# Two mix matmul pairs in place of one behind the operand sums of chunks 4 to 10

## The chip, the cores and the metric

The kernel runs on one core of a Trainium2 chip. Times are device microseconds (us) of one execution. A few executions of each kernel are timed in turn with executions of the kernel before. Kernels with a single timed execution are used for their profiles only. A profile is one further execution, and its times are counted from its first instruction.

Engines are called as the profile calls them: PE (matmuls), PEld (weight loads), DVE (vector engine), ACT (scalar engine), POOL, and SP.

## The reference, cut to what matters

```python
# x: (8, 4224, 192); first a 7-tap causal convolution with softmax weights per head, then:
theta = x @ w_theta
zr, zi = x * np.cos(theta), x * np.sin(theta)
y = einsum('ts,bsd->btd', w_tok_r, zr) + einsum('ts,bsd->btd', w_tok_i, zi)
u = x + y
out = u + np.maximum(u @ w_ch, 0.0)
```

The token mix `einsum('ts,bsd->btd')` is most of the work: 7656 of the 9809 matmuls.

## The kernel before

Tokens are cut into 33 chunks of 128. Each chunk is convolved (PE), copied out of PSUM (ACT), transposed (PE, ACT), multiplied with w_theta (PE), sent through two sine activations (ACT), and made into operands by two products and four sums (DVE). The mix is a stream of pairs of 128x384 matmuls, each pair on one weight tile. The stream consists of steps. A step makes two row blocks of the output from the chunks that are ready (2, 4, 5, 7, 9, then 11), in seven runs that save multiplications in the manner of Strassen and Winograd; the names "11", "S1", "S2", "S4", "S3", "12", "22" are those of the weight tiles.

Chunks 0 to 10 are made at the beginning, in what I call the front. There the stream is not issued in one piece: `between(n)` issues up to n of its pairs between the stages of the chunks.

```python
    for i in range(NW + 2):                 # NW = 11
        ch = chunks.get(i) if i < NW else None
        old = chunks[i - 1] if 0 < i <= NW else None
        ...
        if ch:
            ch.conv(0)
        between(2)
        if old:
            old.theta(0)
        between(1)
        if ch:
            ch.conv(1)
        ...
        ready[0] = i - 2
        between(2)
        if old:
            old.theta(1)
        ...
        between(1)
        if ch:
            ch.transpose()
        if old:
            old.product(Z11)
        between(2)
        ...
        if old:
            old.product(Z21)
        between(1)
        if old:
            old.sums(0)
        between(1)
        if old:
            old.sums(1)
        between(1)
```

The program gives each engine its work in this order of issue. The work that a step of the mix asks of the other engines is issued with its pairs, at positions from 0 to 7 (one per run): weight tiles are turned (L336) and summed (L348) on DVE for the next step, and a finished run is given from PSUM (`y`) to SBUF (`pv`), by a copy on ACT (L406) or an addition on DVE (L408).

```python
    def w_tasks(self):
        ...
            (0.25, lambda: self.turn("11")), (1.2, lambda: self.turn("21")),
            (2.05, lambda: self.wsum("S3")), (2.2, lambda: self.turn("22")),
            (3.05, lambda: self.wsum("S1")), (3.3, lambda: self.wsum("S2")),
            (4.2, lambda: self.turn("12")), (5.1, lambda: self.wsum("S4")),
    ...
    def wtile(self):
        return wpool.tile([P, NW, NQ, Q], F16, name="wt", tag="wt", bufs=9)
    ...
    ypool = ... tc.tile_pool(name="yps", bufs=2, space=bass.MemoryType.PSUM)   # y: 2 tiles of 2 banks
```

Of the kernel before, what the change touches and what calls it, by code (L numbers as in the profile page):

```python
# [16 lines left out]
def kernel(  # L17
# [257 lines left out]
    def load_chunk(k):  # L275
        if k < NK and k not in chunks:
            chunks[k] = Chunk(k, before=chunks[k - 1] if k % NW else None)
# [308 lines left out]
    def idle(n):  # L586
        for _ in range(n):
            pe(nc.tensor.matmul(
                spare[:, 0, 0:BH], lhsT=noise[:, 0:P], rhs=noise, start=True, stop=True
            ))  # L590
# [54 lines left out]
    def more(n):  # L645

        for i in range(n):
            if need[0] is None:
                need[0] = next(flow, NK)
            if need[0] > ready[0]:  # L650
                return n - i
            need[0] = next(flow, NK)
        return 0
# [8 lines left out]
    for i in range(NW + 2):  # L662
        ch = chunks.get(i) if i < NW else None
        old = chunks[i - 1] if 0 < i <= NW else None

        def between(n):
            left = more(n)
            if 0 < i < 3:
                idle(min(left, 2))
# [9 lines that stand above are left out]
        if i == 0:  # L679
            idle(4)  # L680
# [4 lines that stand above are left out]
        if i == 1:  # L685
            for at, f in steps[0].w_tasks():
                if at < 2.2:
                    f()
        if i + 3 < NW:
            load_chunk(i + 3)  # L690
# [6 lines that stand above are left out]
        if i == 1:  # L697
            for at, f in steps[0].w_tasks():
                if at >= 2.2:
                    f()  # L700
        if old:
            old.product(Z21)
        between(1)
        if old:
            old.sums(0)
        between(1)
        if old:
            old.sums(1)
        between(1)
    ready[0] = NK  # L710
    for _ in flow:
        pass
# [31 lines left out]
```

## Time and profile before

| quantity | value | where it is from |
|---|---|---|
| time, median of the first three runs | 1447.86 us (1446.54 to 1449.32) | timed runs |
| span of the profile | 1444.6 us | profile page |
| PE busy | 1414.5 us, 98% | profile page |
| front: from the first theta of chunk 4 to PE's resumption after its last gap | 44.46 to 102.48 us, 58.02 us long | timeline |
| PE busy and DVE busy in that stretch | 51.91 and 51.98 us | table of windows |

The front is the piece that the change touches. It begins with a matmul that stands before the first moved pair, and it ends with a mix matmul that has the same place in PE's order in every kernel (the 774th that is profiled, but for the two kernels that have fewer or more matmuls on purpose).

### The profile page before, as it was taken

The page shows a single profiled execution, that of the slowest core. Times are in us where ns is not written, and L with a number is a line of the kernel's source. Part 1 is how long each engine was busy: PE and PEld are TensorE (multiplying, and loading weights), DVE is VectorE, ACT ScalarE, POOL GpSimd, SP SyncE. Part 2 cuts the span into 40 slices and gives each one's busy share as a digit, 9 for nine tenths or more (in the row PEclk, how much of TensorE's full clock was granted, in tenths as well). Part 3 has the DMA queues.
Part 4 walks back from the last instruction along what each step waited for, and adds up shares of the span by engine and source line. Part 5 has one row for each costly group of instructions (what it writes and reads, how often), then busy time and mean ns, then how long its engine had stood idle before and what let it go on. Part 6 is the DMA issues. An engine that isn't in the chain of part 4 may idle for free.

```text
span 1444.6 us, 23749 instructions
## 1 busy us (share of the span) xinstructions
PE 1414.5 (98%) x9809; PEld 886.3 (61%) x9809; DVE 978.2 (68%) x1050; ACT 316.2 (22%) x379; POOL 434.6 (30%) x655
## 2 busy tenths in 40 slices
PE   7899999999999999999999999999999999999997
PEld 4656666666666666666666666666666666666665
DVE  6893554555448687866666657876877677767686
ACT  6851101111124254000000004435210110010133
POOL 8421211111223232432433343233323123213120
PEclk9999999999999999999999999999999999999999
DMA  9975756564699999897899889989999999898883
GB/s 181 253 148 136 146 119 133 98 152 87 152 229 210 226 244 222 219 265 173 223 245 222 233 155 239 235 181 237 274 220 202 213 204 221 204 200 193 166 232 116
DMA packets 272029, 281.99 MB, mean 195 GB/s; under 512 B 106672, under 2 KB 240176, under 8 KB 271920
## 3 DMA queue, kind: packets, MB, share of 16 engines
q0 software_dynamic: 162464, 92.15, 48.4%
q1 hardware_dynamic: 71824, 178.88, 35.2%
q10 hardware_dynamic: 37632, 9.44, 4.3%
q8 instruction: 77, 1.26, 0.4%
q14 instruction: 32, 0.26, 0.1%
HBM read 245.49 MB, written 108.13 MB: 245 GB/s over the span
## 4 chain that ended last, share of the span: by engine, by line
PE 89%; DVE 3%; DMA 2%; ACT 2%; POOL 1%; issue 1%; SPq 0%; DVEq 0%; ACTq 0%; POOLq 0%
PE y L443 81%; PE v L141 5%; PE pc L210 1%; PE tp L165 1%; ACT z L246 1%; DVE pv L408 1%; DMA xw<-xw 1%; POOL xw L197 1%; DMA xw<-in_x_dram 1%; DVE z L257 1%; POOL st L323 1%; DVE z L251 1%; DMA pv<-part 1%; ACT uT L151 1%; DVE wt L336 0%
## 5 line engine op out<-in xcount | busy, mean ns | idle before, releaser
L443 PE MATMUL y<-z,wt 128*128 128x384 f16 x7656 | 1283.6, 326 | 10.4 <-DVE pv L408 7.3
L443 PEld LDWEIGHTS <-wt 128*128 128x128 f16 x7656 | 740.7, 98 | 488.1 <-issue 10.2
L408 DVE TENSOR_TENSOR pv<-y,pv 128x768 f32<-128x768 f32 x324 | 309.2, 955 | 327.0 <-PE y L443 286.8
L336 DVE STREAM_TRANSPOSE wt<-st 128x1408 f16<-128x1408 f16 (+7 forms) x224 | 327.8, 1465 | 45.8 <-PE y L443 39.1
L323 POOL DMA_DIRECT2D st<-in_moe_w_tok_r_dram x232 | 132.4, 579 | 464.9 <-DVE wt L336 459.4
L323 POOL DMA_DIRECT2D st<-in_moe_w_tok_i_dram x232 | 132.5, 580 | 405.4 <-DVE wt L336 397.5
L348 DVE TENSOR_TENSOR wt<-wt 128x1408 f16<-128x1408 f16 (+7 forms) x216 | 176.1, 815 | 40.5 <-PE y L443 38.0
L151 ACT ACTIVATE z<-pc 128x768 f16<-128x768 f32 x65 | 53.3, 820 | 386.7 <-PE pc L210 386.5
L151 ACT ACTIVATE ub<-pv 128x768 f16<-128x768 f32 x63 | 50.2, 835 | 333.2 <-DVE pv L408 310.7
L406 ACT ACTIVATE pv<-y 128x768 f32<-128x768 f32 x66 | 54.0, 819 | 281.6 <-PE y L443 281.6
L141 PEld LDWEIGHTS <-uT 128*128 128x128 f16 x1056 | 91.1, 98 | 27.4 <-issue 8.5
L386 POOL TENSOR_TENSOR pv<-pv,xr 128x1536 f32<-128x1536 f32 x24 | 74.5, 3105 | 67.1 <-DVE pv L476 21.9
L197 POOL DMA_DIRECT2D xw<-in_x_dram x132 | 76.5, 591 | 30.1 <-DMA xw<-xw 9.7
L476 DVE SCALAR_TENSOR_TENSOR pv<-v,pv 128x768 f32<-128x768 f32 x66 | 62.9, 954 | 27.5 <-PE v L141 27.0
L151 ACT ACTIVATE uT<-tp 128x1536 f16<-128x1536 f16 (+1 forms) x49 | 59.7, 1221 | 74.4 <-PE tp L165 74.4
L257 DVE TENSOR_TENSOR z<-z 128x768 f16<-128x768 f16 x132 | 73.4, 556 | 3.6
L246 ACT ACTIVATE z<-v,half_pi 128x768 f16<-128x768 f32 x66 | 59.9, 907 | 42.1 <-PE v L141 41.7
L251 DVE TENSOR_TENSOR z<-z 128x1536 f16<-128x1536 f16 x66 | 60.1, 948 | 6.6 <-ACT z L246 6.6
L141 PE MATMUL v<-wth,uT 128*128 128x192 f16 x528 | 55.0, 248 | 5.6 <-ACT z L246 3.3
L141 PE MATMUL v<-wch,uT 128*128 128x192 f16 x528 | 54.2, 246 | 2.1 <-DVE pv L476 1.2
L246 ACT ACTIVATE z<-v 128x768 f16<-128x768 f32 x66 | 53.5, 810 | 0.0
L210 PE MATMUL pc<-xw,bands 96*64 96x192 f16 x528 | 35.3, 256 | 1.2 <-DVE bands L628 0.8
(43 smaller groups left out, 138.0 us busy)
## 6 DMA issues: line engine op xcount, KB each, us to landing
part<-pv SPq DMA_DIRECT2D x79, 768.0 KB, 4.6
pv<-part SPq DMA_DIRECT2D x79, 768.0 KB, 6.0
out_dram<-pv SPq DMA_DIRECT2D x66, 384.0 KB, 4.3
st<-in_moe_w_tok_r_dram POOLq DMA_DIRECT2D x136, 176.0 KB, 5.7
st<-in_moe_w_tok_i_dram POOLq DMA_DIRECT2D x136, 176.0 KB, 5.1
xs<-z SPq DMA_DIRECT2D x132, 96.0 KB, 4.1
xw<-in_x_dram POOLq DMA_DIRECT2D x121, 96.0 KB, 5.9
xr<-xs SPq DMA_DIRECT2D x24, 384.0 KB, 4.5
```

The lines of the kernel that those rows point to most:

```text
L141: pe(nc.tensor.matmul(v[:, k, b * D : (b + 1) * D], lhsT=tT[:, 3 * k + b + i, :], rhs=w[:, 2 * b + i, :], start=(i == 0), stop=(i == 1),))
L151: act(nc.scalar.activation(out=out, in_=in_, func=AT.Copy))
L197: nc.gpsimd.dma_start(out=self.xw[lo : lo + n, h, :, :], in_=x[:, t0 : t0 + n, :].rearrange("b s d -> s b d"),)
L246: act(nc.scalar.activation(**args))
L251: dve(nc.vector.tensor_tensor(out=o, in0=xv, in1=o, op=ALU.mult))
L257: dve(nc.vector.tensor_tensor(out=z[:, o, :], in0=z[:, a, :], in1=z[:, b, :], op=ALU.subtract))
L323: pool(nc.gpsimd.dma_start(out=st[a * Q : (a + 1) * Q, 0:nb, :, 0:n] .rearrange("i r bt s -> i (r bt) s"), in_=w[self.tbs[0] * P : (self.t ...
L336: dve(nc.vector.transpose(self.w[name][:, 0 : self.n, :, :], self.st[int(name[1])][:, int(name[0]) - 1, :, 0 : self.n * Q] .rearrange("p b ...
L348: dve(nc.vector.tensor_tensor(out=self.w[name][:, 0 : self.n, :, :], in0=self.w[a][:, 0 : self.n, :, :], in1=self.w[b][:, 0 : self.n, :, : ...
L386: ins = pool(nc.gpsimd.tensor_tensor(out=self.pv[i], in0=self.pv[i], in1=self.xr[i], op=ALU.add))
L408: dve(nc.vector.tensor_tensor(out=o, in0=yv, in1=o, op=ALU.add))
L443: pe(nc.tensor.matmul(y[cn][:, q, 0:BH], lhsT=self.w[wn][:, c, :, :].rearrange("p bt i -> p (bt i)"), rhs=chunks[k].z[:, zn, q * BH : (q + ...
```

## The change

The intent is to fill PE's idle time in the front: while DVE forms the operand sums, PE gets two mix pairs to do in place of one.

```diff
         between(1)
         if old:
             old.sums(0)
-        between(1)
+        between(2 if i > 4 else 1)
         if old:
             old.sums(1)
-        between(1)
+        between(2 if i > 4 else 1)
```

No instruction is added or removed.

## The prediction

> **What bounds the kernel now.** I read the whole-kernel shares first, to see how much there is to win at all.
>
> ```profile
> PE 1414.5 (98%) x9809; PEld 886.3 (61%) x9809; DVE 978.2 (68%) x1050; ACT 316.2 (22%) x379; POOL 434.6 (30%) x655
> PE 89%; DVE 3%; DMA 2%; ACT 2%; POOL 1%; issue 1%; SPq 0%; DVEq 0%; ACTq 0%; POOLq 0%
> ```
>
> PE is busy for 1414.5 of 1444.6 us, so all its idle time is 30.1 us, 2.1% of the span. The change reorders instructions and removes none, so that is the outer ceiling. The second question is how much of it lies where the change acts. That is the front: chunks 0 to 10 are convolved, turned, rotated by theta and multiplied, with mix matmul pairs (two 128x384 matmuls on one weight tile) strewn between. By the timeline, the iteration that makes chunk 5 and finishes chunk 4 has its turn at 47.97 us and the last front theta at 90.58. The table of windows:
>
> ```profile
> 48.00:102.48 54.48, 48.86 (x434) 32.33 (x432) 49.19 (x70) 43.01 (x53) 15.60 (x28) 1.00 0.97 205
> 103.00:1444.60 1341.60, 1328.99 (x9034) 829.64 (x9032) 894.96 (x918) 240.64 (x286) 382.33 (x554) 1.00 0.87 195
> ```
>
> Columns: window, its length, then PE, weight load, DVE, ACT, POOL busy. From 48 to 102.48 us PE is busy 48.86 of 54.48: 5.6 us idle, 0.39% of the run. Everything after 103 us keeps its instructions and order. So only these 5.6 us are in play, and I looked at which waits make them. PE's rows of the timeline (whole ones with a gap over 0.4 us):
>
> ```profile
> 51.92 0.48 PE L443 MATMUL y<-z,wt 128*128 128x384 f16 x2 [0.61 <-ACT pv L406]
> ...
> 61.12 0.48 PE L443 MATMUL y<-z,wt 128*128 128x384 f16 x2 [0.99 <-DVE pv L408]
> ...
> 83.80 0.81 PE L443 MATMUL y<-z,wt 128*128 128x384 f16 x4 [0.48 <-DVE pv L408]
> ...
> 87.32 1.78 PE L443 MATMUL y<-z,wt 128*128 128x384 f16 x10 [0.41 <-DVE pv L408]
> ...
> 102.48 5.70 PE L443 MATMUL y<-z,wt 128*128 128x384 f16 x34 [2.31 <-DVE pv L408]
> ```
>
> Four of the five end with a vector addition that clears a PSUM tile (y), the last and longest one when the front is already over: DVE still works off its backlog and PE waits for it. So near the end of the front the bound is DVE, and I read its rows for idle time:
>
> ```profile
> 57.65 0.84 DVE L336 STREAM_TRANSPOSE wt<-st 128x640 f16<-128x640 f16 x1 [1.42 <-PE y L443]
> ...
> 80.06 1.11 DVE L336 STREAM_TRANSPOSE wt<-st 128x896 f16<-128x896 f16 x1 [1.43 <-PE y L443]
> ...
> 93.72 1.78 DVE L251 TENSOR_TENSOR z<-z 128x1536 f16<-128x1536 f16 x2
> ...
> 101.47 0.95 DVE L408 TENSOR_TENSOR pv<-y,pv 128x768 f32<-128x768 f32 x1
> ```
>
> From 80.06 to 102.34 DVE has no visible gap. Its last gap, 1.43 us, is a wait for the mix itself: the weight turn "12" needs a weight buffer (of nine) that is free only when the mix has ended its S3 run.
>
> [...] DVE and ACT are the front's busy ones (49.2 and 43.0 of 54.5 us, DVE without a gap after 80 us), PE the later bound, and the gaps of 1.42 and 1.43 us are waits for a weight buffer. [...] So a blocked turn "12" holds up all products behind it, as at 80.06, and it is the order that is being changed here. [...]
>
> **The change, part by part.** Added and removed work: none; the listing of both programs has 19620 PE rows each. Moved: one pair later in the stream is issued behind each of two sums, 2 extra pairs for each of chunks 4 to 10. Against the old order, the convolution of chunk 6 comes 2 pairs later, of chunk 7 4, of chunk 10 10, and the last thetas (chunk 10) 12. (The pairs placed after chunk 10's own sums have only mix behind them anyway.) A pair takes 2 x 0.164 us (ten matmuls in the row of 1.79 us less the last one's tail), so 0.33 us, and by the end of the front 12 x 0.33 = 3.9 us of mix has moved ahead of theta. It is not saved; it fills idle PE time or pushes the front later.
>
> (a) What DVE regains. In the new order the turn "12" of the 7-chunk step stands behind the products and two sums of chunk 7, and S3 ends in the chunk 9 iteration right after its first convolution, while in the old order it ended after that iteration's turn of the operand. I estimate S3's end at about 76 us and DVE's arrival at 77.5 (old 78.6, less two sums of 0.56). So the gap of 1.43 us goes, if nothing else delays DVE. The gap of 1.42 us at 57.65 stays: S3 of the step before ends at the same row (850) in both orders.
>
> (b) What DVE loses. Theta comes later, so the sines do, so the products may wait. Chunk 10: the last theta began at 90.58, its last sine ended at 93.6, and DVE took the product at 93.72, so there is hardly any slack. With 3.9 us more mix ahead and about 1.5 of the 3.1 us idle that PE showed in between recovered, theta begins at about 93.0 and the first half's sines are done about 95.2. DVE comes there at 93.72 - 1.43 + 2.05 (a weight sum of 0.75 and a turn of 1.30 now stand ahead of it) = 94.3, and waits about 0.8.
>
> (c) The end of the backlog. After that DVE has two products (1.75), two weight sums (1.54), four sums (2.3) and the addition (0.87), together 6.5 us: 95.2 + 6.5 = 101.7, against 102.34 before. Without the wait of (b) it is 100.9. PE itself arrives earlier (100.17 minus what idle it fills), but it must wait for this addition, because the pair that opens run "12" needs its bank. So PE resumes 0.6 to 1.4 us earlier, and everything behind it shifts by as much. Gain: about 1.0 us, 1447.86 - 1.0 = 1446.8.
>
> **Rivals.**
> 1. PE-bound front: all idle is filled, because the extra pairs stand exactly where PE waits for ACT. For it: 5.6 us idle. Against: 2.3 of these are the DVE backlog, whose work before that addition is the same in both orders, and the waits for y at 61, 83.8 and 87.3 are DVE's too. It would give 1443 to 1444.
> 2. ACT-starved front: the delay of convolution and theta reaches the sines and DVE loses more than (a) gives. For it: ACT already waits for theta (0.6 us at 60.16 and 63.51, 0.85 at 89.80) and DVE's slack at chunk 10 is 0.1 us. Against: the pairs are put at the end of an iteration, where ACT still has sines and a turn of 1.45 us in hand. It would give 1448 to 1450.
> 3. A transfer: one load of x now stands behind a weight load that waits for a turn (issued about 61 in place of 53.6 us, for a convolution after 73). With about 6 us to land and 4.7 for the halo copy it is still in time; no effect.
>
> **Range and chances.** The three runs before spread from 1446.5 to 1449.3, so half of my range is noise. The mechanism allows -4 to +2 us. Range 1443.8 to 1449.6. 2% is 29 us, five times all the idle time in play, so both verdicts beyond it get 1% and "same" gets 98%.
>
> **What would show it.** Right: PE idle from 48 us to the end of the front's backlog is 4 to 5 us instead of 5.6; DVE has no gap of over 1 us near 78 to 80; the last PE gap, before run "12" of the 9-chunk step, still ends with DVE's addition, which finishes between 100.9 and 101.7; DVE now waits for ACT's sine at chunk 9 or 10; all after 103 us is as it was. Step (a) is wrong if a wait of over 1 us for a weight buffer shows again; (b) is wrong if ACT is never waited for, or for over 2 us; the whole is wrong if the time changes by more than 4 us, which would need another cause behind 103 us, such as a new repeating wait in the mix.

That a blocked turn holds up the product behind it is shown in the trace at 80.06: this product began at 81.09 us, though the last sine that it reads had ended at 78.98.

## The result, and the profile after

The first timed runs gave 1451.76 us (1451.63 to 1453.93, four runs) against 1447.91 us for the kernel before (1446.54 to 1449.32, four runs). The ratio is 1.0030, with a 95% interval from 1.0013 to 1.0047. A ratio here is the mean time of one kernel's runs over that of the other's of the same rounds, so it isn't quite the ratio of the medians quoted. The result is clearly slower, but well inside 2%, and it lies above my range.

First the shares of the changed kernel, from its page:

```profile
PE 1417.1 (98%) x9809; PEld 887.9 (61%) x9809; DVE 978.1 (67%) x1050; ACT 316.6 (22%) x379; POOL 435.2 (30%) x655
PE 88%; DVE 5%; DMA 2%; ACT 2%; issue 1%; POOL 1%; SPq 0%; DVEq 0%; ACTq 0%; POOLq 0%
```

The same instructions have much the same busy time, and DVE's share of the chain that ended last rose from 3% to 5% of the span. Next comes the table of windows: the front and the rest of the kernel before, then the same two stretches of the changed kernel. The columns are the window, its length, then busy time (and instructions) of PE, PEld, DVE, ACT and POOL, PE's granted clock, DMA share and GB/s.

```profile
44.46:102.48 58.02, 51.91 (x463) 34.54 (x463) 51.98 (x75) 46.32 (x57) 17.12 (x30) 1.00 0.99 212
102.48:1444.60 1342.12, 1329.51 (x9036) 829.96 (x9036) 895.48 (x918) 240.64 (x286) 382.33 (x554) 1.00 0.87 195
```

```profile
46.34:106.87 60.53, 51.99 (x462) 34.24 (x463) 52.00 (x75) 46.69 (x57) 17.35 (x31) 1.00 0.96 204
106.87:1449.70 1342.83, 1329.67 (x9036) 829.95 (x9036) 895.40 (x918) 240.63 (x286) 382.68 (x554) 1.00 0.87 195
```

The two spans differ by 5.1 us (1449.7 - 1444.6). Of these, 1.88 us lie before the first moved instruction (46.34 - 44.46), 2.51 us in the front, and 0.71 us behind it. In the front PE and DVE work as long as before within 0.1 us (51.99 and 52.00 us), so the 2.51 us are idle time on both. PE's idle time in it did not fall from 6.1 us as intended; it rose to 8.5.

PE's timeline of the changed kernel, the mix rows with a gap over 0.7 us (start, duration, what, and in brackets the gap and what ended it):

```profile
53.80 0.48 PE L443 MATMUL y<-z,wt 128*128 128x384 f16 x2 [1.17 <-ACT pv L406]
...
62.62 0.81 PE L443 MATMUL y<-z,wt 128*128 128x384 f16 x4 [1.34 <-DVE pv L408]
63.36 0.52 PE L210 MATMUL pc<-xw,bands 96*64 96x192 f16 x8
...
71.62 0.48 PE L443 MATMUL y<-z,wt 128*128 128x384 f16 x2 [0.79 <-ACT pv L406]
...
106.87 8.30 PE L443 MATMUL y<-z,wt 128*128 128x384 f16 x50 [3.89 <-DVE pv L408]
```

Before, the first two gaps were 0.61 and 0.99 us and there was none at the place of the third. So the extra pairs did not fill idle time there. They came sooner to the point where the stream has to wait for its own PSUM tile, and the convolution behind them (63.36) waited too. From there to the last gap no other gap of PE is over 0.3 us, and the last gap grew from 2.31 to 3.89 us.

DVE's timeline, every row with a gap over 0.5 us from 56 to 106 us, and the addition that ends the front:

```profile
60.02 0.84 DVE L336 STREAM_TRANSPOSE wt<-st 128x640 f16<-128x640 f16 x1 [1.92 <-PE y L443]
...
68.86 0.96 DVE L251 TENSOR_TENSOR z<-z 128x1536 f16<-128x1536 f16 x1 [0.89 <-ACT z L246]
...
77.84 1.83 DVE L251 TENSOR_TENSOR z<-z 128x1536 f16<-128x1536 f16 x2 [0.84 <-ACT z L246]
...
93.24 0.96 DVE L251 TENSOR_TENSOR z<-z 128x1536 f16<-128x1536 f16 x1 [1.93 <-ACT z L246]
...
105.86 0.95 DVE L408 TENSOR_TENSOR pv<-y,pv 128x768 f32<-128x768 f32 x1
```

The 1.43 us for a weight turn near 80 us are gone, as predicted. In their place there are waits for ACT's sines at chunks 6, 7 and 9 (0.89, 0.84 and 1.93 us), and the turn of the step before waits 1.92 in place of 1.42 us. The sum is -1.43 + 0.50 + 3.66 = +2.73 us, which accounts for the front's 2.51; the small gaps left out of the sum make the difference.

ACT shows the link between the two. Its row of the convolution behind the stalled pair:

```profile
63.92 0.81 ACT L151 ACTIVATE z<-pc 128x768 f16<-128x768 f32 x1 [2.29 <-PE pc L210]
```

ACT idled for 2.29 us because the convolution was stuck behind a mix pair. The sines are queued behind this row, and DVE's product at 68.86 is waiting for them. (The last of these sines, at 67.93, itself waited 0.25 us for theta, which PE worked on behind the same stalled pair. At chunks 7 and 9 the last sine stood directly behind a copy of a mix tile on ACT; by my estimate, theta alone would have let it start about 0.35 us earlier each time: it ended at 76.49 and 91.89 us, the sines began at 76.88 and 92.29, and the one at 67.93 began 0.04 us after its theta.)

### The profile page after: what moved, and what is told of

Read it like the earlier page. It is cut to its first block, busy times and chain, and to the rows that moved or that the text cites. A ratio compares the mean times of both kernels' runs of the same rounds, so it can differ in the third digit from the quotient of the medians.

```text
span 1449.7 us, 23749 instructions
## 1 busy us (share of the span) xinstructions
PE 1417.1 (98%) x9809; PEld 887.9 (61%) x9809; DVE 978.1 (67%) x1050; ACT 316.6 (22%) x379; POOL 435.2 (30%) x655
## 4 chain that ended last, share of the span: by engine, by line
PE 88%; DVE 5%; DMA 2%; ACT 2%; issue 1%; POOL 1%; SPq 0%; DVEq 0%; ACTq 0%; POOLq 0%
PE y L443 80%; PE v L141 5%; PE pc L210 2%; PE tp L165 1%; DVE pv L408 1%; DVE z L257 1%; ACT z L246 1%; DMA st<-in_moe_w_tok_i_dram 1%; DVE wt L336 1%; DVE z L251 1%; DMA xw<-in_x_dram 1%; DVE wt L348 1%; DMA xw<-xw 1%; DVE pv L476 0%; POOL st L323 0%
```

## The experiments

The theories, as the expectations name them:

- **Theory A**: the pairs ahead of convolution and theta make the sines late; DVE waits for them, and PE waits for DVE's last addition.
- **Rival B**: the loss is mostly a difference of start-up.
- **Rival C**: the two collisions of the early chunks (PE gaps of 1.17 and 1.34 us) are the whole loss.
- **Rival D**: what counts is the place of the pairs against the waits for PSUM tiles, not the lateness.
- **Theory E**: the loss is one chain that starts at the weight turn "12", which stands in DVE's queue before a buffer that the mix has yet to free.

The table gives all 16 runs beside the two profiles. "Front" is the stretch defined above, "DVE waits" the sum of DVE's gaps over 0.3 us in it, and "last theta" is the second theta of chunk 10, counted from the start of the front.

| kernel | front us | DVE waits us | last theta us |
|---|---|---|---|
| before / same | 58.02 / 58.01 | 4.66 / 4.65 | 46.11 / 46.11 |
| after / after_again | 60.54 / 60.54 | 7.39 / 7.39 | 50.94 / 50.95 |
| early | 58.75 | 5.30 | 48.49 |
| late | 57.16 | 4.25 | 48.08 |
| moved | 60.33 | 7.38 | 48.42 |
| elsewhere | 59.05 | 5.83 | 49.48 |
| fewer | 57.98 | 4.47 | 43.76 |
| first / last | 61.06 / 61.08 | 7.58 / 7.59 | 50.80 / 50.82 |
| late12_a | 60.64 | 7.17 | 51.04 |
| late12_b / late12_b_timed | 56.30 / 56.29 | 2.58 / 2.58 | 44.49 / 44.48 |
| late12_fewer | 58.54 | 4.87 | 43.32 |
| late12_late | 56.43 | 3.22 | 47.35 |
| after_light | 58.44 | 5.29 | not comparable |
| before_heavy | 58.63 | 5.00 | 46.72 |

Front less DVE waits is between 52.9 and 53.7 us in every row. In part this is bookkeeping: a stretch is as long as one engine's work and gaps together, and DVE works 51.7 to 52.3 us in every front. What makes DVE the engine to look at is the end of the front: in 17 of the 18 profiles PE then waits for DVE's addition (in `fewer` PE gets there without a gap). So **DVE's waits are the part of the front that the place of the pairs changes**; why they arise is for the experiments to show. Last theta alone doesn't tell the length: `moved` has an earlier one than `early` and is 1.6 us longer.

The front repeats to 0.02 us between profiles of one program, while whole times scatter by 2 us and more.

### after_again and same: what repeats

`after_again` is the changed kernel and `same` is the kernel before; neither has an edit.

> The changed kernel once more, to part what the change does from what the start-up does. In the first profile 1.88 us of the loss lay before the first moved instruction (theta at 46.34 in place of 44.46 us), with the start-up's small matmuls at 2.64 in place of 1.57 us, and DVE's idle time after that grew from 4.66 to 7.39 us (+2.7). Theory A (the extra pairs delay convolution and theta, ACT's sines come late, DVE's queue starves and PE waits for DVE's last addition): from the theta of chunk 4 to PE's resumption after the last gap it again takes 60.5 us, against 58.0 before, and the median is 2.5 us slower than before. Rival B (mostly a start-up difference): that stretch repeats, but the median comes within 1 us of before when the start-up is like that of before. If the start-up is systematically late, the median is again 4 us slower.

> The kernel before, unchanged, as a kernel of its own: what the time and the start-up scatter when nothing is changed. Expected ratio 1.000 within 0.001. Theory A expects 58.0 us from the theta of chunk 4 to PE's resumption; the start-up (up to that theta) may differ by 1 to 2 us from the first profile's 44.46.

Measured: `after_again` 1451.93 us (1451.38 to 1453.84, five runs), `same` 1449.20 (1447.56 to 1450.60, five runs), and before 1448.75 (1446.67 to 1451.01, nine runs). The ratios are 1.0023 (1.0011 to 1.0036) and 0.9998 (0.9984 to 1.0011). The fronts are 60.54 and 58.01 us, exactly as in the first profiles. So 2.5 us of the loss are the change's own, and Rival B falls as the main cause. The start-up is scatter: the first theta of chunk 4 came at 44.46 and 45.48 us in the two profiles of the kernel before, at 46.34 and 45.65 in those of the changed one, and between 44.3 and 45.8 in all the others. The medians differ by 3.2 to 3.9 us; what lies beyond the front's 2.5 is within the scatter, and no run shows a cause for it that belongs to the change.

A second source of scatter shows in `same`. The table of windows around its last PE gap:

```profile
100.40:103.80 3.40, 1.09 (x7) 0.48 (x6) 3.19 (x5) 0.00 (x0) 0.00 (x0) 1.00 0.13 21
103.80:107.20 3.40, 3.40 (x13) 1.65 (x11) 2.42 (x3) 0.00 (x0) 2.18 (x4) 0.51 0.23 19
107.20:110.60 3.40, 3.40 (x23) 2.01 (x21) 2.94 (x3) 0.67 (x1) 0.10 (x1) 0.99 1.28 194
```

After its gap of 2.31 us PE ran for 3.4 us at half the clock (the 0.51): 13 matmuls in place of 23 in the next stretch, which is up to 1.7 us lost (an estimate, half of 3.4 us). The profile of before, with the same gap, has no such stretch, nor has the first one of the changed kernel with 3.89 us; `after_again` has one (a mean clock of 0.73 from 107 to 111 us). So the length of the gap does not decide it.

The gap of 3.89 us in the changed kernel and the 3.4 us behind it, both at a clock of 1.00:

```profile
102.98:106.87 3.89, 0.00 (x0) 0.00 (x1) 3.79 (x8) 0.00 (x0) 0.00 (x0) 1.00 0.01 2
106.87:110.27 3.40, 3.40 (x21) 2.07 (x22) 3.40 (x4) 0.00 (x0) 1.88 (x4) 1.00 0.15 11
```

No rule comes out of this: a gap of 1.71 us in `last` was followed by 3.4 us at a clock of 0.50, and one of 1.93 us in `elsewhere`, which ended at 65.55 us, by a clock of 1.00 up to 73 us. What decides it is not shown.

### early and late: which chunks

```diff
-        between(2 if i > 4 else 1)            # both places
+        between(2 if 4 < i < 7 else 1)        # early
+        between(2 if i > 6 else 1)            # late
```

> Only chunks 4 and 5 get two pairs in place of one. In the changed kernel the two PE stalls of 1.17 us (for ACT's copy) and 1.34 us (for DVE's addition) came right behind these pairs, with ACT idle for 2.29 us. Rival C (these collisions with the opening of a PSUM tile are the whole loss): about +2.5 us, as the whole change. Theory A (the lateness adds up chunk by chunk and is felt at chunks 7 and 9): at most +1 us, with DVE's gaps of 0.84 and 1.93 us at chunks 7 and 9 smaller or gone.

> Only chunks 6 to 10 get two pairs. Rival C: no loss, as the front up to chunk 6 is that of before (PE gaps 0.61 and 0.99, no ACT gap of 2.29). Theory A: +1 to +2 us, DVE waits for ACT's sines by over 1 us at chunk 8 or 9, and PE's last gap is over 3 us (2.31 before, 3.89 with the whole change).

Measured: `early` 1448.97 us (1447.37 to 1450.84, five runs, ratio 1.0002, 0.9989 to 1.0015), front +0.73 us. `late` 1448.39 us (1446.84 to 1448.44, five runs, ratio 0.9992, 0.9980 to 1.0005), front -0.86 us. Rival C falls as the whole loss: `early` has the same two PE gaps and loses only 0.7.

```profile
51.91 0.48 PE L443 MATMUL y<-z,wt 128*128 128x384 f16 x2 [1.17 <-ACT pv L406]
...
60.73 0.81 PE L443 MATMUL y<-z,wt 128*128 128x384 f16 x4 [1.34 <-DVE pv L408]
```

Theory A's number for `late` was wrong, too. Late pairs alone do what the change was meant to do: no wait for a weight turn is left near 80 us, and the one new wait for a sine, at chunk 9, is shorter:

```profile
58.60 0.85 DVE L336 STREAM_TRANSPOSE wt<-st 128x640 f16<-128x640 f16 x1 [1.42 <-PE y L443]
...
89.08 1.83 DVE L251 TENSOR_TENSOR z<-z 128x1536 f16<-128x1536 f16 x2 [1.03 <-ACT z L246]
```

This is close to my step (a) with a wait of the size of step (b), though at chunk 9, and the gain of 0.86 us in the front lies where I had predicted it for the whole change; the ratio of the times doesn't tell it from none. The parts don't add up: +0.73 - 0.86 is not +2.51. What the early pairs leave behind, a mix stream that is four pairs further on and a theta that is late, meets the later pairs; that is my reading, and no run tests it. The last theta shows where its own lateness comes from: four early pairs (1.3 us) make it 2.38 us later than before, eight late ones (2.6 us) only 1.97.

### moved, elsewhere, fewer and first: amount or place

```diff
# moved: the change, and one pair less behind each convolution
-        between(2)                            # behind conv(0), and behind conv(1)
+        between(1 if i > 5 else 2)
# elsewhere: before, and one pair more there
+        between(3 if i > 5 else 2)
# fewer: before, and behind both sums
-        between(1)
+        between(0 if i > 4 else 1)
# first: before, and behind sums(0) only
+        between(2 if i > 4 else 1)
```

> The two extra pairs behind the sums of chunks 5 to 10 stay (chunk 4 too), but each of the two gaps behind the convolutions of the same iterations gives up one pair, so that the mix is not further ahead of convolution and theta than before, beyond two pairs. Theory A (lateness that adds up): the front stretch, from the theta of chunk 4 to PE's resumption, is 58.0 us or less (60.54 in the changed kernel), and DVE's gap of 1.93 us at chunk 9 is gone. Rival D (the place: pairs behind the sums wait for ACT's copy or DVE's addition of the PSUM tile that they go on with): it stays at 59.5 us or more, with PE gaps for pv of over 1 us.

> Two extra pairs in each iteration as in the change, but behind the two convolutions of chunks 6 to 10 and not behind the sums. Theory A: the same lateness for theta, so about 60 us or more for the front stretch (58.0 before, 60.54 changed), and DVE waits of 1 to 2 us for ACT's sines at chunk 9. Rival D: under 58.5 us, as no pair is added where ACT's turn of 1.45 us blocks the copies.

> The mirror: no pair at all behind the sums of chunks 4 to 10 in place of one (before) or two (changed). Theory A: convolution and theta come earlier, ACT never starves and DVE never waits for a sine, so DVE's queue is bound by its own work: but the mix is 12 pairs behind, so the waits of DVE for the mix (1.42 and 1.43 us before) grow to over 2 us each. Front stretch between 57 and 59 us, measured up to the same instruction. If theta's lateness were the only thing, it would be under 56.5.

> One extra pair behind the first pair of sums only: half the change, 6 pairs in place of 12 ahead of the last theta. Theory A, with a slack that is used up before the loss begins (early chunks alone gave +0.7 us, late chunks alone -0.9, together +2.5): little or no loss, 57.2 to 58.5 us for the front stretch. Were the loss proportional to the pairs, it would be 59.3 us.

Measured fronts: 60.33, 59.05, 57.98 and 61.06 us, from one look each. Theory A in its simple form missed three of the four, and in `fewer` it had the length but not the waits. Rival D was right for `moved` (60.33 us, with a PE gap of 1.76 us for an addition) and wrong for `elsewhere`. In `moved`, theta is 2.5 us earlier than in the changed kernel and the front is as long, because DVE now waits twice for the weight turn "12" (1.91 and 1.95 us) and once for a sine (1.29). In `fewer`, theta comes 2.35 us earlier than before and nothing is won: DVE waits 1.97 us for the mix in a weight sum. `elsewhere` loses 1.0, not 2, us. And `first`, with half the extra pairs, loses more than the whole change, but with a halved clock in its front (a mean of 0.97 from 44 to 100 us; next section). DVE's rows for the weights, one of `moved` and one of `fewer`:

```profile
83.51 1.11 DVE L336 STREAM_TRANSPOSE wt<-st 128x896 f16<-128x896 f16 x1 [1.95 <-PE y L443]
...
56.60 0.49 DVE L348 TENSOR_TENSOR wt<-wt 128x640 f16<-128x640 f16 x1 [1.97 <-PE y L443]
```

So in these runs DVE waits on two sides: for sines with the mix further ahead (3.66 us in the changed kernel), and for weight buffers with it further behind (1.97 us in `fewer`).

### last: half the pairs once more

```diff
             old.sums(1)
-        between(1)
+        between(2 if i > 4 else 1)            # behind sums(1) only
```

> The extra pair behind the second pair of sums in place of the first. PE and DVE get the same order of instructions as with the pair behind the first sums (checked on the listings), so this repeats that run, whose front was 61.06 us with a stretch of halved clock inside it (67.1 to 69.6 us). Expected 59.5 to 60 us without such a stretch: half the pairs cost as much as all of them, so the loss does not go by the number of pairs. If it is 58.5 or less, the clock alone made that run long.

Measured: 61.08 us, within 0.02 us of `first`, from one look. The halved clock repeats as well. PE's timeline of `last`, and its table of windows:

```profile
65.68 0.48 PE L443 MATMUL y<-z,wt 128*128 128x384 f16 x2 [1.71 <-DVE pv L408]
66.01 1.12 PE L141 MATMUL v<-wth,uT 128*128 128x192 f16 x8
```

```profile
66.40:69.80 3.40, 3.40 (x23) 2.53 (x21) 1.95 (x3) 2.26 (x3) 0.00 (x0) 0.50 1.26 343
```

A wait of 1.71 us for an addition on DVE was followed by 3.4 us at half clock (0.50), with theta inside it taking 1.12 in place of 0.82 us. Up to 1.7 us of the lateness can come from the clock (an estimate, as above). PE, DVE and ACT have the same order of instructions in `first` and `last`, so this is one kernel twice and not a second split. My expectation of 59.5 to 60 us was made for a case that did not occur, and whether half the pairs would cost less without the halved clock stays open.

### late12_a, late12_b and late12_fewer: the turn that blocks DVE

```diff
-                (4.2, lambda: self.turn("12")), (5.1, lambda: self.wsum("S4")),
+                (5.05 if self.t < 6 else 4.2, lambda: self.turn("12")),
+                (5.1, lambda: self.wsum("S4")),
...
-                found.append((1.3 + 3 * (m - 1), lambda m=m: nxt.load_w(m)))
+                found.append((1.3 + (3.77 if t < 5 else 3) * (m - 1), lambda m=m: nxt.load_w(m)))
```

The edit is made to the changed kernel (a), to the kernel before (b), and to `fewer`.

> The changed kernel with the weight turn "12" of the front's steps put behind the end of run S3 (5.05 in place of 4.2 of a step's 7 parts; its load of the next weights moves along), so that DVE does not stand before a weight buffer that the mix has yet to free. Theory E (the loss of the early pairs is a chain: turn "12" waits 1.92 us for the mix, the addition behind it comes late, PE waits 1.34 us for that addition, the convolution behind it is late, ACT idles 2.29 us, DVE waits 0.89 us for chunk 6's sine): all five waits go or shrink to under half and the front stretch falls from 60.54 to 59 us or less. Theory A (theta is late only because of the 3.9 us of pairs ahead of it): the waits at chunks 7 and 9 stay or take over, and the stretch stays within 0.5 us of 60.5.

> The kernel before with the same shift of turn "12". Its two DVE gaps for that turn, 1.42 and 1.43 us, should go. If the front is as long as DVE's work plus DVE's waits, as nine profiles show so far, the stretch falls from 58.0 to 55.5 to 57 us; if the waits only move to the sines, it stays at 58.

> No pairs behind the sums of chunks 4 to 10, and turn "12" shifted. With theta at its earliest and no block by the turn, DVE's waits should be the fewest of all kernels: front to the same matmul 55.5 to 57 us (58.0 before). If the mix is then too far behind and DVE waits for it in other weight sums or additions, it stays over 57.5.

Measured fronts: 60.64, 56.30 and 58.54 us. Theory E falls, and Theory A's number for `late12_a` holds, though not all of its waits. In `late12_a` the two waits that it names at the head of the chain are gone, the 1.92 us of DVE for the turn and PE's 1.34 us, yet the front is as long as before the edit. The waits moved, as DVE's timeline shows:

```profile
58.99 0.96 DVE L251 TENSOR_TENSOR z<-z 128x1536 f16<-128x1536 f16 x1 [1.53 <-ACT z L246]
...
76.74 0.63 DVE L348 TENSOR_TENSOR wt<-wt 128x896 f16<-128x896 f16 x1 [2.15 <-PE y L444]
...
92.70 0.96 DVE L251 TENSOR_TENSOR z<-z 128x1536 f16<-128x1536 f16 x1 [1.68 <-ACT z L246]
```

On the old order the same edit does win. All of DVE's rows of `late12_b` with a gap over 0.3 us in the front:

```profile
50.30 1.83 DVE L251 TENSOR_TENSOR z<-z 128x1536 f16<-128x1536 f16 x2 [1.81 <-ACT z L246]
57.74 1.83 DVE L251 TENSOR_TENSOR z<-z 128x1536 f16<-128x1536 f16 x2 [0.38 <-ACT z L246]
79.32 1.83 DVE L251 TENSOR_TENSOR z<-z 128x1536 f16<-128x1536 f16 x2 [0.39 <-ACT z L246]
```

Its waits of 1.42 and 1.43 us for the turn are gone, with two of 0.38 and 0.39 for sines in their place, so DVE waits 2.08 us less, and the front is 1.72 us shorter. `late12_fewer` missed the 55.5 to 57 us; its other branch came true, as DVE's wait of 1.97 us for the mix in a weight sum stays.

### after_light and before_heavy: PE time ahead of theta

```diff
# after_light: the change, and theta of chunks 5 to 10 with half its matmuls
-                for i in range(2):
+                for i in range(1 if light else 2):
# before_heavy: before, and 12 more matmuls in conv(0) of chunks 6 to 10
-            for h in range(4):
+            for h in [0, 1] * more + list(range(4)) * (1 + more):    # more: j == 0 and 6 <= k < NW
```

> The changed order of instructions on ACT and DVE, but theta of chunks 5 to 10 has half its matmuls (8 in place of 16 a chunk, 0.65 us less PE time, as much as the two extra pairs add; the result is wrong on purpose). Theory A (PE time ahead of theta makes the sines late): the DVE waits for the sines at chunks 6, 7 and 9 (0.89, 0.84, 1.93 us) shrink to under 1 us in all and the front stretch falls from 60.54 to 58.5 us or less. Rival D (the order of the pairs against the waits for PSUM tiles): the PE waits for pv of 1.17, 1.34 and 0.79 us stay or grow and the stretch stays at 59.5 us or more.

> The old order of the mix, but the first convolution of each of chunks 6 to 10 does its matmuls 2.5 times (12 more of about 0.057 us, 0.68 us a chunk, as much as two pairs; the result stays right). Theory A: theta is late by up to 3.4 us as it is with the extra pairs, DVE waits for sines, and the front stretch grows from 58.0 to 60 us or more. Rival D: PE's idle time takes it up in part (5 us of it), no new waits for pv, 59 us or less.

Measured: `after_light` has a front of 58.44 us (60.54 in the changed kernel), as Theory A said and Rival D denied. PE's gaps stay, 1.17, 1.34, 0.57 and 0.76 us, but the waits for the sines shrink; DVE's timeline:

```profile
66.92 0.96 DVE L251 TENSOR_TENSOR z<-z 128x1536 f16<-128x1536 f16 x1 [0.56 <-ACT z L246]
75.57 1.83 DVE L251 TENSOR_TENSOR z<-z 128x1536 f16<-128x1536 f16 x2 [0.51 <-ACT z L246]
...
90.14 0.96 DVE L251 TENSOR_TENSOR z<-z 128x1536 f16<-128x1536 f16 x1 [1.10 <-ACT z L246]
```

Together they are 2.17 in place of 3.66 us (over the 1 us that I had expected). Its result is wrong in principle, because half of theta's sum is left out, but the comparison still called it correct: with these inputs the error stays within its tolerance. It is no candidate. One control is missing: the kernel before with the same half theta. So how much of the 2.1 us is loss undone, and how much any order would gain from about 4 us less PE work (twelve thetas, each 0.49 in place of 0.82 us), is not shown.

`before_heavy` missed what Theory A expected (60 us or more) and came out as Rival D expected (59 or less): 58.63 us, only 0.61 more than before. It has 2.5 us more PE work ahead of theta (from its start to the next row, each of the five convolutions takes 0.95 in place of 0.45 us; I had expected 0.68 us more, from 0.45 us for eight matmuls, and it was 0.50), and yet its last theta is only 0.61 us later (46.72 against 46.11). PE's idle time took up the rest: of the gaps of 0.61, 0.99, 0.48 and 0.41 us only one of 0.50 is left until the last one, and DVE waits for no sine beyond that of chunk 4 which every kernel has; its turn waits 1.78 in place of 1.43 us. The row of PE and the row of DVE:

```profile
61.09 0.48 PE L443 MATMUL y<-z,wt 128*128 128x384 f16 x2 [0.50 <-DVE pv L408]
...
80.64 1.11 DVE L336 STREAM_TRANSPOSE wt<-st 128x896 f16<-128x896 f16 x1 [1.78 <-PE y L443]
```

So added PE time as such is mostly absorbed; added mix pairs were not, for their last theta was 4.83 us later for 3.9 us of pairs. The two fillers don't stand at the same places, though, and the first is smaller by 1.4 us. Together the two runs support what neither theory said alone: the loss takes the late theta (the sine waits shrink with it), and theta becomes that late because the extra pairs run into waits of their own instead of into idle time. The second half is read from the PE gaps of 1.17, 1.34 and 0.79 us; no run removed them and kept the pairs.

### late12_b_timed and late12_late: a shorter front than either

`late12_b_timed` is `late12_b`, timed; `late12_late` is that edit together with the one of `late`.

> The old order with the weight turn "12" of the front put behind run S3, which had a front of 56.3 us against 58.0 in its one profile. Expected 1.7 us faster than before in the front, the same behind it: ratio 0.9988 (between 0.997 and 1.000)[...].

> Turn "12" shifted and two pairs for chunks 6 to 10 only. Alone these gave 56.3 and 57.16 us (58.02 before). If both took away the same DVE wait (1.43 us at the 7-chunk step's turn), together they give no more than the first: 56.3 to 57.5 us. If they add up, 55.5 us.

Measured: `late12_b_timed` 1447.39 us (1446.55 to 1447.57, six runs) against 1449.23 (1447.60 to 1455.57, eleven runs), ratio 0.9985 (0.9970 to 1.0000). Its front is 56.29 us. `late12_late` 1447.85 us (1445.27 to 1449.74, six runs), ratio 0.9984 (0.9967 to 1.0002), front 56.43. The two edits take away the same wait and do not add up. The moved turn is thus better than both kernels in its front, by 1.7 us against before and 4.2 us against the change, while its whole time is not clear of noise, with an interval that ends at 1.000.

## Why the prediction was wrong

**The frame held.** The change is within 2%, the time in play was only the front, the last PE gap still ends with DVE's addition, and everything behind the front is as before (1342.83 against 1342.12 us, with the same busy times). That DVE's chain ends the front was right, and held in 17 of 18 profiles. But calling DVE and ACT the front's busy engines was a poor reading of my own line: PE's 48.86 us of the 54.48 lie beside DVE's 49.19. The kept order of a queue, on which I had counted, shows in the traces (the convolution at 63.36 directly behind its pair, which stalled for 1.34 us).

**Step (a) held in one half.** The wait of 1.43 us for the turn "12" of the 7-chunk step went (in `late` too, where DVE waits for no sine over 0.3 us between the two turns). The one of the 5-chunk step, which I said stays at 1.42, became 1.92. I had compared its place in PE's order, which is the same, but not the PE waits ahead of it.

**Step (b) failed, and with it the sign.** The sentence is "about 1.5 of the 3.1 us idle that PE showed in between recovered". Nothing was recovered. The last theta came 4.83 us later for 3.9 us of pairs, so the idle time ahead of it grew by 0.9 us; my term was off by 2.4 us. PE stood 1.17 us for an ACT copy that was queued behind a transposed operand, 1.34 us for DVE's addition, and 0.79 us for a copy again, with the next convolution behind it each time. In the following iterations PE had hardly a gap, and 13 pairs in place of 11 lengthened one of them from 7.13 us (73.47 to 80.60) to 7.75 us (79.69 to 87.44). The waits for sines were then 3.66 us at chunks 6, 7 and 9, not 0.8 us at chunk 10. At chunk 10, where I had looked for the wait because its slack was smallest, there is none: the earlier waits had made DVE late enough.

**Step (c) held in form.** The front's end follows DVE's waits, but they were 2.73 us more and not fewer, so PE resumed 2.51 us later and not 0.6 to 1.4 us earlier. The rest of the 3.2 to 3.9 us between the medians is of the size of the scatter in start-up and clock.

**The rivals.** Rival 2 of the prediction was the right one in mechanism, and too small. What I held against it, that ACT has a turn of 1.45 us in hand at the end of an iteration, turned out to be the reason for two of the stalls (1.17 and 0.79 us): the copy that the pair needed stood behind that turn. Rival 1 (idle time simply filled) is refuted by PE's idle time in the front, 8.5 against 6.1 us. Rival 3 had no effect that a wait of PE, ACT or DVE in the front shows.

**What stays open.** Why `early` and `late` together cost 2.5 us and singly +0.73 and -0.86 is seen only as different waits in different places. No run gives a rule that tells beforehand where a pair will meet a tile's release. Nor did I get a profile of the first or the last pair without the halved clock, or run the kernel before with half of theta.

## What to carry to other kernels

Before filling idle time of an engine, ask whether the filler waits for the same engines that caused the idle time. Here an independent filler of 2.5 us was mostly absorbed (the last theta came 0.61 us later), while dependent pairs of 3.9 us delayed the last theta by 4.8 us (one profile of the first and two of the second, with the filler at different places). In a stage like this one, where a stalled instruction held up its queue on several engines (a pair on PE for 1.34 us, a turn on DVE for 1.92), add up the waits of the engine whose work is fixed, and try to move what blocks its queue (here one weight turn, 1.7 us won in the front) rather than push more work into another. Then measure again: in the changed order the same move won nothing (60.64 us), because the waits went elsewhere.
